# Six neighbouring tokens to a partition, mask columns by matrix product, and a new instruction order in a block-sparse attention and feed-forward kernel

## The chip, the cores and the metric

The kernel runs on one core of a Trainium2 chip. The metric is the device time of one execution in microseconds (us), taken as the median of several runs. The core has five engines that work side by side, each through its own instructions in order: TensorE (PE), VectorE (DVE), ScalarE (ACT), GpSimd (POOL) and SyncE (SP), which issues most transfers. Data lie in an on-chip memory of 128 partitions; products are summed in a second memory, PSUM.

## What is computed

Attention over 4 batches, 8 heads, 768 tokens and 64 dimensions a head, with a mask over blocks of 32 tokens, and behind it a feed-forward layer of 512 x 2048 x 512 over all 3072 tokens:

```python
block = 32; n_blocks = S // block                     # 24
scores = np.matmul(q, k.transpose(0, 1, 3, 2)) / np.sqrt(D)
mask = np.abs(blk_i - blk_j) <= 1                     # neighbours
mask = mask | (blk_i == 0) | (blk_j == 0) | (blk_i == n_blocks - 1) | (blk_j == n_blocks - 1)
for qb in range(n_blocks):
    for kb in sampled_blocks[qb]:                     # three drawn blocks per row of blocks
        mask[qb*block:(qb+1)*block, kb*block:(kb+1)*block] = True
attn = softmax(np.where(mask, scores, -1e9))
x = (attn @ v).transpose(0, 2, 1, 3).reshape(B * S, H * D)
h = x @ w_in
out = (h * sigmoid(beta * h)) @ w_out
```

## The kernel before, in words

**Loads.** Two heads form a pair, so there are 16 pairs, four per batch; x numbers them. For each pair the loads of k, q and v bring 2 x 768 rows of 64 float32 values into staging tiles `st_k`, `st_q`, `st_v` (384 KB each, `add_load`, line 473). The 768 tokens of a batch are split into three groups of 256 (`NG`), and in each group partition p gets the two neighbouring tokens 2p and 2p + 1 (`CG = 2`). A partition thus reads runs of 2 x 64 x 4 = 512 bytes. Token chunk c (of `NC = 6`, 128 tokens each, one per partition) is the even or odd half of a group. All orders within a batch follow these chunks: the columns of the transposed k and q (`kX`, `qX`), those of x, and the rows of the output that one store writes (`add_store`, line 784).

The first four pairs are loaded in pieces: pair 0's k in three parts (k0a, k0b, k0c), every q in a first part of 256 tokens (q0 to q3) and a rest of 512 (r0 to r3, two transfers each). The order on SP is fixed by `ORDER` (line 128): k0a q0 k0b k0c v0 k1 q1 v1 k2 q2 v2 k3 q3 v3 r0 r1 r2 r3. The weights w_in and w_out come in two halves each through POOL's queue (`add_weights`, line 443); the first half of w_in is held back until k3 has landed. The loads of pair 4 (k4, q4, v4) wait for halves of w_out.

**Casts and transposes.** Staged tiles are cast to float16 by DVE or POOL (`add_cast`, line 504). k and q are then transposed by PE, with a copy from PSUM by DVE or ACT (pairs 0 to 3), or by a transposing transfer from SP (later pairs).

**Units of attention.** A unit is one pair with 256 or 512 queries; there are 32, in the order of tiles of a batch. For a unit, PE forms the scores of key chunks into `sc`, ACT takes the exponential into `et` (tiles of 128 x 1024), DVE multiplies by the mask (`mk` in `tile_steps`, line 608), PE forms the product with v (`av`), DVE normalizes into `xst`. A multiply leaves out the columns of blocks of queries that see every key. In the first four units (`N_PEMASK`) PE adds the mask instead, by a product of `onehot` with `shut_qk`, and there is no multiply. x is transposed to `x` by PE in the first eight units and by transfers later.

**Mask.** `emit_first` (line 320) and `add_mask` (line 366) build a 24 x 24 table of blocks, `mask16`, from `sampled_blocks`. PE multiplies it with the identity; ACT spreads the 24 columns to 384 in `shut_qk`; DVE copies the 24 x 24 table to `mask_t`; three products with `onehot` give `mask_kb` (128 x 72); and three copies ("spread") repeat each column into `mask01` (128 x 3 x 384), which the multiplies read.

**Feed-forward.** Seven groups of tokens (256, five of 512, 256): hidden products `hp`, tanh on ACT (`t_sb`), a multiply on DVE (`g`), output products, copies or sums into `osb`, stores. Six groups use a scheme of seven products on sums of quarter matrices (`add_mixed`), for which DVE makes sums `s` and mixed weights `w_mix`.

**Order.** All instructions are emitted in the order of the string `STEPS` (line 42), one word per node: the node's number, its engine (P, A, D, G for POOL, S for SP) and the buffers it takes; "2V7" stands for two dummy products of 512 columns into bank 7 and W for 64 columns. A planner outside the kernel found this order with the durations that stand in the `add` calls. Those numbers do nothing at run time. Each engine runs its nodes strictly in this order, and waits wherever data or buffers aren't there.

Of the kernel before, what the change touches and what calls it, by code (L numbers as in the profile page):

```python
# [10 lines left out]
FP32 = mybir.dt.float32  # L11
FP16 = mybir.dt.float16
# [11 lines left out]
class Node:  # L24


    def __init__(self, kind, eng, dur, lat, emit, deps=(), take=(), use=(), moved=0,
                 rows=128, port=False, at=0.0, place=0.0, part=0, lanes=1):
# [14 lines left out]
11S0 15S0 19S 23S 27S0 12D0 0D 29S1 13P0 2V7 3W7 33S1 14A0 37S1 16D0 17P1 39S2 9P0 20G 1P2 1V7  # L43
43S2 10D 2A 3D 18D 4P3 24D 21P0 80P2 22D 5D 25P2 82P3 81A0 8G 26D 84P0 28D0 83A1 47S0 85A2
49S3 30D1 53S0 34G1 31P6 7G 35P7 86P0 32D1 36A 91P1 87D0 38D1 93P2 92A3 88D0 57S1 95P3 40D2
89P1 59S1 44D2 94A4 41P0 45P2 42D2 63S2 46A 90D0 96A5 48G2 102P2 104P1 6D 103A6 97P6 50D3 75G
105A7 54D0 51P7 76G 98D1 67S0 55P4 99D1 106P0 52D3 77G 56D 107A8 113P1 115P3 60D1 114A9 100P0
71S1 117P2 64D2 116Aa 61P1 101D 108P2 62D 68G0 118Ab 184P3 58G3 109D2 187P0 110D2 69P3 185Ac
190P2 78G 70D 65P2 111P3 188Ad 66D 193P3 79G 119P2 191Ae 186D 196P0 189D 194A0 199P2 112D
120D3 192D 197A1 210P3 121D3 195D 122P3 200A2 213P0 123D 198D 216P1 211A3 124P4 201D 127P5  # L50
214A4 212D 202P6 125A0 130P7 215D 128A1 205P0 217A5 203D4 126D0 129D 133P1 204D4 131A2 136P4
206D5 218D 134A3 219P1 137A4 139P5 207D 220A6 132D 142P0 138D 145P6 135D 140A5 72D1 148P4
143A6 141D 151P1 146A0 144D 222P1 149A1 147D 73P0 152A2 150D 154P5 223A7 74D 157P4 221D 225P3
155A4 224D 160P0 158A3 226A8 163P2 153D 159D 166P3 156D 208P1 161A5 227D 247P3 236G0 164A6
169P4 167A0 162D 237S 228P5 209D1 248A9 168D 165D 250P0 170A1 229D6 231P3 249D 251Aa 171D
253P3 230D0 232D7 256P0 254Ab 233D 259P2 172P2 252D 257A0 255D 178P3 260A1 258D 262P3 240G2
281P0 367D 173P 263A2 244G0 241S 363D 284P2 282Ac 245S 368D 287P3 179P 364D 285Ad 238D0 174P
283D 288Ae 239S0 264D 290P0 293P2 261D 296P3 291A3 175P 273S1 289D 294A4 234P0 265P1 242D0
176A0 292D 243S 180P 297A5 295D 181P 286D 276S0 298D 279S1 268P2 182A1 266D8 246G0 235D 307S2
267D1 299P6 269D9 365D 302P3 274G1 300Da 270D 301D2 404P2 303Db 275S1 407P0 304D 271P2 405A6  # L60
305P3 272D 410P3 306D 408A7 177S 413P2 369D 315P2 366D 411A8 318P3 409D 316A2 277D2 321P6
414A0 406D 278S 317D1 280G1 416P0 319A3 419P2 324P7 415D 322A4 310S1 313S0 308G2 417A1 323D
327P2 412D 309S2 420A2 330P6 418D 325A5 320D 333P0 429S3 328A0 326D 432S2 336P1 331A6 329D
334A1 437P2 421D 440P1 337A2 339P7 332D 311G1 438A9 335D 422P6 312S 338D 441Aa 342P0 423Dc
371D0 340A4 443P2 424D3 343A3 446P1 439D 345P1 444Ab 341D 430G3 348P6 442D 346A5 431S3 344D
314G2 449P2 447A3 351P7 445D 435S1 450A4 354P0 448D 349A0 347D 433G0 452P1 352A6 462P2 350D
425P1 434S 453A5 353D 357P6 451D 355A1 426Dd 360P7 454D 463Ac 427D 465P1 356D 358A2 428S2
468P2 455P1 361A4 359D 466Ad 458P0 362D 456De 469Ae 471P3 457D4 474P1 459Df 464D 377P1 472A0
460D 372D 477P2 475A1 380P0 473D 470D 478A2 487P3 490P1 476D 381P 488A6 479D 493P2 467D 491A7
496P3 378P 374D 494A8 375D 480P2 370D 379A0 483P3 497A3 481Dg 382D 499P2 482D0 388P 484Dh  # L70
500A4 485D 502P3 593P1 596P2 503A5 385P 594A9 386P 597Aa 599P3 606P1 619S0 622S0 625S0 623G2
436G3 620D0 492D 495D 498D 501D 504D 489D 389P 600Ab 383D 505P4 607A0 376D 373D 609P3 387A
612P1 506D0 508P5 595D 610A1 507D1 391P 601D 613A2 509D1 510D 627P3 640S1 183S 643S1 461S 486S
646S1 641G1 630P1 598D 628Ac 633P2 392P 384D 631Ad 390D1 644G1 602P6 634Ae 394P 603D2 626D0
604D2 648P1 661S2 621S0 664S2 511S 624S 667S0 393D 651P2 654P3 649A3 642S1 395P 635D 608D
652A4 512P2 396D 655A5 662D2 515P3 665D0 513A3 669P2 682S3 605S0 672P3 516A5 518P0 514D0 645S
517D 521P2 519A0 632D 663S2 670A6 650D 524P3 653D 685S0 397P 522A6 520D 683G3 525A1 523D 527P4
526D 666S 530P0 614D 528A2 629D 673A7 398P 401S 611D 531A4 675P1 399D 690P3 533P5 676A8 532D
403S 684S3 671D 691A9 615P1 677D 693P1 534A3 529D 686G2 696P3 636P0 694Aa 535D 536P4 647D1
697Ab 616D3 668D2 539P5 687S 692D 537A5 617D3 703P1 656D 540A0 706P3 542P1 538D 704A0 674D  # L80
545P4 543A6 637D4 560D0 548P2 638D4 546A1 544D 639S 551P3 549A4 541D 554P0 561D 688S1 552A2
547D 402S 707A1 557P1 550D 709P2 555A3 553D 716P3 657P2 558A5 556D 710A2 559D 678P3 658D5
717Ac 659D0 719P0 679D6 722P2 566P2 680D1 720Ad 563D 698D 567P 723Ae 695D 810P3 564D 813P0
816P2 811A3 569P3 721D 711D 814A4 699P6 568D1 689G3 817A5 570P 700D7 708D 819P0 701D2 822P2
705D 825P3 820A6 574P 571D 823A7 724D 712P0 573D 826A8 577P 713D8 714D4 572D 835P2 860S0 400S
863S1 702S 660S 866S0 838P3 841P0 718D 836A9 578P 562D 839Aa 827D 725P4 579D0 864G1 842Ab 575P
726D9 861G0 727D2 844P3 847P0 824D 850P2 845A0 583P 565D 576A 815D 584P 848A1 812D 580P 843D
851A2 821D 868P3 893S1 715S 681S 896S2 862S0 728S 618S 871P0 894D1 874P2 869Ac 581P 899S1 818D
897G0 872Ad 828P6 582D 875Ae 831P7 585D 829Da 849D 877P0 880P2 729P3 832Db 878A3 830D0 833D
732P6 879D 730A6 881A4 586P 731D1 852D 733A0 883P0 901P2 926S2 834S1 895S1 840D 735P3 884A5  # L90
927D2 734D 902A6 738P7 867D0 587P 736A1 885D 737D 904P0 588A 907P2 846D 741P6 739A4 592S 882D
929S0 744P3 740D 742A2 898S 837D 747P2 745A3 743D 591S 905A7 853P7 746D 590S 932S0 870D 750P6
748A5 928S2 854Dc 855D4 856P3 751A6 876D 589S 753P7 908A8 873D 865S 749D 910P0 754A0 913P2
752D 756P2 911A0 930D2 857Dd 759P6 858D 914A1 903D 762P3 755D 757A1 777D0 760A4 765P4 763A2
758D 768P5 766A3 761D 771P2 906D 769A5 767D 774P7 772A6 764D 886P4 773D 775A0 770D 916P0
1015P1 1040S3 1041G3 887De 889P6 917A2 776D 900G1 1042S3 783P5 1016A9 890Df 912D 931S 1018P0
909D 1021P1 784P 1019Aa 888D1 780D 859S 1022Ab 786P4 918D 891D 785A0 1024P0 781D 892S 1027P1
1030P3 1025A3 915D 787P 782D 1043S1 1028A4 919P0 778D 1031A5 922P1 920Dg 921D2 1048P1 923Dh
1051P3 924D 791P 1049Ac 788D 925S 1026D 1052Ad 1054P0 1057P1 1023D 794P 1055Ae 1050D 792P 790D
1058A0 1044G0 1060P3 793D 1063P0 1073P1 1061A1 933G2 795P 1045S 1020D 1064A2 934P6 1029D  # L100
1074A6 1032D 937P7 1053D 935A1 940P2 938A4 936D0 943P3 941A3 779D 1076P0 942D 944A2 946P6
1077A7 945D 949P2 1017D 947A6 952P3 789D 950A5 1075D 955P0 953A0 948D 1033P1 796D1 956A1 939D
# [899 lines left out]
```

## Time and profile before

| | |
|---|---|
| three runs | 267.02, 267.15, 277.67 us; median 267.15 |
| profiled execution | span 268.4 us from first to last instruction; the profile gives no other time of it |
| mean granted TensorE clock | 0.991 |
| busy in 0 to 25 us | PE 17.39, DVE 12.35, ACT 16.06, POOL 8.30 |
| busy in 25 to 44 us | PE 18.30, DVE 17.32, ACT 17.44, POOL 2.25 |
| 384 KB loads, issue to landing (median) | k 4.4, q 4.1, v 4.1 us |
| 128 KB parts of q | 5.4 us |
| halves of w_in, w_out | 12.4, 13.1 us |
| packets of SP's queue | 69744, 32.06 MB, 50.2% of 16 engines' span |
| last matmul ends | 264.7 us |

In the lines of the profile a group is named by its operation and its tiles, "out<-in"; in brackets stands how long the engine was idle before it and which engine, tile or transfer ended that. Nearly all instructions carry line 186, that of a helper which records them, so groups are told apart by their tiles. POOL's casts have line 510 and loads lines 481 and 484.

### The profile page before, as it was taken

What the parts mean: (1) busy time and instruction counts of PE and PEld (TensorE: products, weight loads), DVE (VectorE), ACT (ScalarE), POOL (GpSimd) and SP (SyncE); (2) the same over time, 40 slices, a digit from 0 to 9 for tenths busy, and PEclk for the clock granted to TensorE, in tenths of its full rate; (3) what the DMA queues carried; (4) which work ended last, traced back from release to release, by engine and by line L of the source; (5) the groups of instructions that cost most, each with busy time, mean ns of one, the idle gap of its engine ahead of it and who ended that gap; (6) DMA issues with size and microseconds to landing.
All of it is one profiled execution on the core that took longest, in us unless ns stands there. A gap on an engine that the chain in (4) does not pass through costs nothing.

```text
span 268.4 us, 6856 instructions
## 1 busy us (share of the span) xinstructions
PE 254.6 (95%) x2774; PEld 166.2 (62%) x2774; DVE 233.1 (87%) x492; ACT 209.7 (78%) x277; POOL 33.0 (12%) x49
## 2 busy tenths in 40 slices
PE   7793899999999899999999999999999999999994
PEld 3672675463456575646776546655667875578883
DVE  5662899999999999999998999999999788986582
ACT  3894899959999888899899898997478988564420
POOL 3234001021603200201201002020000000000000
PEclk9998899999999999999999999999999999999999
DMA  6999995297949779928189496620016012102042
GB/s 191 297 242 215 209 222 142 58 255 187 217 109 288 155 172 212 210 50 254 23 215 169 123 256 104 139 41 0 32 53 176 15 7 84 26 2 78 2 156 78
DMA packets 72978, 36.68 MB, mean 137 GB/s; under 512 B 29796, under 2 KB 68980, under 8 KB 72948
## 3 DMA queue, kind: packets, MB, share of 16 engines
q1 hardware_dynamic: 69744, 32.06, 50.2%
q0 software_dynamic: 3136, 4.19, 9.0%
q8 instruction: 21, 0.34, 0.5%
q14 instruction: 9, 0.07, 0.1%
q10 hardware_dynamic: 68, 0.01, 0.0%
HBM read 27.27 MB, written 6.29 MB: 125 GB/s over the span
## 4 chain that ended last, share of the span: by engine, by line
PE 75%; DVE 16%; DMA 3%; ACT 2%; SPq 1%; issue 1%; POOL 0%; DVEq 0%; POOLq 0%
PE sc L186 75%; DVE et L186 6%; DVE g L186 4%; DMA st_q<-in_q_dram 3%; DVE xst L186 2%; ACT et L186 1%; SPq L484 1%; DVE s L186 1%; DVE w_out_sb L186 1%; DVE recip L186 1%; DVE osb L186 0%; POOL s_q L510 0%; DVE s_k L186 0%; ACT shut_qk L186 0%; DVE s_q L186 0%
## 5 line engine op out<-in xcount | busy, mean ns | idle before, releaser
L186 ACT ACTIVATE et<-sc 128x1024 f16<-128x1024 f32 x144 | 139.8, 1037 | 19.9 <-PE sc L186 19.1
L186 PE MATMUL sc<-x,w_in_sb 128*128 128x512 f16 (+1 forms) x448 | 90.8, 349 | 0.4 <-ACT et L186 0.2
L186 ACT ACTIVATE t_sb<-sc,beta_c_sb 128x512 f16<-128x512 f32 (+1 forms) x112 | 67.6, 647 | 22.4 <-PE sc L186 19.6
L186 DVE TENSOR_TENSOR et<-et,mask 128x960 f16<-128x960 f16 (+1 forms) x132 | 83.2, 660 | 1.2 <-ACT et L186 1.0
L186 DVE SCALAR_TENSOR_TENSOR g<-t_sb,sc 128x512 f16<-128x512 f16 (+1 forms) x112 | 63.5, 603 | 2.7 <-ACT t_sb L186 2.4
L186 PEld LDWEIGHTS <-w_in_sb 128*128 128x128 f16 x448 | 41.5, 98 | 38.0 <-issue 6.1
L186 PEld LDWEIGHTS <-g 128*128 128x128 f16 x483 | 45.4, 98 | 17.3 <-issue 7.5
L186 PE MATMUL sc<-w_out_sb,g 128*128 128x256 f16 (+1 forms) x384 | 51.2, 282 | 0.0
L186 PE MATMUL sc<-qX,kX 64*128 64x256 f16 (+1 forms) x384 | 46.2, 329 | 0.7 <-DVE qX L186 0.3
L186 PEld LDWEIGHTS <-et 128*128 128x128 f16 x1152 | 41.4, 98 | 7.5 <-issue 2.8
L186 PE MATMUL sc<-va,et 128*128 128x65 f16 x1152 | 43.6, 194 | 0.6 <-ACT et L186 0.3
L186 PEld LDWEIGHTS <-kX 64*128 64x128 f16 x384 | 16.0, 94 | 17.8 <-issue 13.3
L186 PE MATMUL sc<-w_mix,s 128*128 128x256 f16 x176 | 22.2, 273 | 0.7 <-DVE osb L186 0.7
L186 DVE TENSOR_TENSOR xst<-sc,recip 128x256 f16<-128x256 f32 x48 | 19.9, 418 | 0.8
L186 PEld LDWEIGHTS <-s 128*128 128x128 f16 x176 | 16.2, 98 | 5.5 <-issue 3.4
L186 DVE TENSOR_TENSOR osb<-osb,sc 128x512 f32<-128x512 f32 (+1 forms) x18 | 11.3, 635 | 6.1 <-ACT osb L186 3.2
L186 ACT COPY osb<-sc 128x512 f32<-128x512 f32 (+2 forms) x16 | 9.0, 562 | 9.2 <-PE sc L186 7.9
L510 POOL CAST s_q<-st_q 128x768 f16<-128x768 f32 (+2 forms) x10 | 9.6, 960 | 50.5 <-DMA st_q<-in_q_dram 37.7
L510 POOL CAST s_k<-st_k 128x768 f16<-128x768 f32 (+1 forms) x8 | 7.0, 877 | 51.0 <-DMA st_k<-in_k_dram 51.0
L186 DVE RECIPROCAL recip<-sc 128x4 f32<-128x4 f32 x48 | 8.3, 175 | 5.1 <-PE sc L186 4.8
L510 POOL CAST va<-st_v 128x768 f16<-128x768 f32 x9 | 9.3, 1029 | 23.4 <-DMA st_v<-in_v_dram 23.4
L186 PE MATMUL sc<-w_mix,g 128*128 128x256 f16 x88 | 11.1, 272 | 0.0
(65 smaller groups left out, 107.6 us busy)
## 6 DMA issues: line engine op xcount, KB each, us to landing
st_v<-in_v_dram SPq DMA_DIRECT2D x16, 384.0 KB, 4.1
out_dram<-osb SPq DMA_DIRECT2D x23, 256.0 KB, 2.3
st_k<-in_k_dram SPq DMA_DIRECT2D x15, 384.0 KB, 4.4
st_q<-in_q_dram SPq DMA_DIRECT2D x12, 384.0 KB, 4.1
w_in_sb<-in_moe_w_in_dram POOLq DMA_DIRECT2D x2, 1024.0 KB, 12.4
w_out_sb<-in_moe_w_out_dram POOLq DMA_DIRECT2D x2, 1024.0 KB, 13.1
st_q<-in_q_dram SPq DMA_DIRECT2D x12, 128.0 KB, 5.4
st_k<-in_k_dram SPq DMA_DIRECT2D x3, 128.0 KB, 2.4
```

The lines of the kernel that those rows point to most:

```text
L186: r = f(*a, **kw)
L484: nc.sync.dma_start(out=o[:, g::NG], in_=hg[:, g::NG])
L510: e(out=at(dst)[:, :, :, 0:D] if nm == "v" else by_chunk(dst, lo, hi), in_=src)
```

## The change

A partition gets six neighbouring tokens of a batch, 6p to 6p + 5, and chunk c is the c-th of them. A full load so reads one run of 1536 bytes per head and partition; a part of two chunks 512, and a rest of four chunks 1024 bytes in one transfer instead of two. Chunks 2g and 2g + 1 of a partition lie in the same block of 32 tokens, so the mask is a function of partition and g (`onehot[:, g]`).

`onehot` is made by POOL in token order in a scratch tile and copied by DVE into the order of g. The product of `mask16` is now with `onehot` itself and gives 384 columns; from it come `shut_qk` (128 columns, as only g = 0 is needed) and `mask_q` (24 x 384), and three products of `onehot` with `mask_q` give the three parts of `mask01`, copied from PSUM by ACT or DVE. `mask_t`, `mask_kb` and the spreads go. A multiply leaves out the first and last four partitions' queries in every chunk: 120 of 128 columns, so 960 elements for 256 queries (before 896) and 960 for 512, with a further level in the access pattern.

Stores write the rows of one chunk, each 2048 bytes, at a distance of six tokens instead of two.

`STEPS` is new throughout. Node numbers rise by one behind the mask. In the new order 19 casts go from DVE to POOL, two from POOL to DVE, eight PSUM copies of the output from DVE to ACT and two from ACT to DVE.

The diff also brings code for splitting products into two halves of the rows (`halves`, `products`, the branches on `HALVED` and `HALVED_AV`). Both switches are empty, and none of it is emitted.

```diff
-11S0 15S0 19S 23S 27S0 12D0 0D 29S1 13P0 2V7 3W7 33S1 14A0 37S1 16D0 17P1 39S2 9P0 20G 1P2 1V7
-43S2 10D 2A 3D 18D 4P3 24D 21P0 80P2 22D 5D 25P2 82P3 81A0 8G 26D 84P0 28D0 83A1 47S0 85A2
...
+12S0 16S0 20S 24S 28S0 0D 30S1 21G 34S1 17D0 5V7 2W7 1P0 13G0 18P1 25G 38S1 3A 14P2 2A 3W7 26P3
+15D0 22P4 40S2 19A 27D 6P5 23A 8P6 29D0 7A 44S2 85P0 9A 83P1 48S0 86A0 10P7 31D1 50S3 4P4 35D1
...
+HALVED_AV = False
+HALVED = ()
...
             nc.gpsimd.tensor_copy(
-                out=onehot[r].rearrange("b g (m r) -> b (g m) r", r=BLK // CG),
+                out=onehot_n[r].rearrange("b p g -> b (p g)").rearrange(
+                    "b (m r) -> b m r", r=BLK // CG),
...
+        nc.vector.tensor_copy(out=onehot, in_=onehot_n.rearrange("b p g -> b g p"))
...
-            pe.matmul(at(tb)[:, 0:NB], lhsT=mask16.rearrange("b h j -> b (h j)"),
-                      rhs=identity[0:NB, 0:NB], start=True, stop=True)
+            pe.matmul(at(tb)[:, 0:NG * P], lhsT=mask16.rearrange("b h j -> b (h j)"),
+                      rhs=onehot[0:NB].rearrange("b g p -> b (g p)"), start=True, stop=True)
...
-            copy_on(eng)(out=mask_t, in_=at(tb)[0:NB, 0:NB])
...
+            copy_on(eng)(out=mask_q, in_=at(tb)[0:NB, 0:NG * P])
+
+        def km(g, kb):
+            pe.matmul(at(kb)[:, 0:NG * P], lhsT=onehot[0:NB, g], rhs=mask_q, start=True, stop=True)
+
+        def kmc(eng, g, kb):
+            copy_on(eng)(out=mask01[:, g], in_=at(kb)[:, 0:NG * P])
...
-        def spread(eng, g):
...
-            hg = src[b, 2 * j:2 * j + 2].rearrange("h (g p c) d -> p (h g) (c d)", g=NG, p=P)
-            o = at(st).rearrange("p h (g c) -> p (h g) c", g=NG)
-            if hi - lo == NC:
-                nc.sync.dma_start(out=o, in_=hg)
-            else:
-                for g in range(lo // CG, hi // CG):
-                    nc.sync.dma_start(out=o[:, g::NG], in_=hg[:, g::NG])
+            rows = src[b, 2 * j:2 * j + 2].rearrange("h (p c) d -> p h (c d)", c=NC)
+            nc.sync.dma_start(out=at(st)[:, :, lo * D:hi * D], in_=rows[:, :, lo * D:hi * D])
...
-        lo, hi = BLK // CG * (q0 == 0), n // CG - BLK // CG * (q0 + n == S)
-        masked = 2 * CG * kn * (hi - lo)
+        lo, hi, ng = 4, P - 4, n // (CG * P)
+        masked = 2 * CG * kn * ng * (hi - lo)
...
-                e = at(et).rearrange("p h (r q) -> p (h r) q", q=w)[:, :, lo:hi]
-                m = mask01[:, kc0 // CG, q0 // CG + lo:q0 // CG + hi].unsqueeze(1).to_broadcast(
-                    [P, 2 * CG * kn, hi - lo])
+                e = at(et).rearrange("p h (r g q) -> p (h r) g q", g=ng, q=P)[:, :, :, lo:hi]
+                m = mask01[:, kc0 // CG, q0 // CG:(q0 + n) // CG].rearrange(
+                    "p (g q) -> p g q", q=P)[:, :, lo:hi].unsqueeze(1).to_broadcast(
+                        [P, 2 * CG * kn, ng, hi - lo])
...
-            rows = out[b * S:(b + 1) * S, :].rearrange("(g p c) m -> g c p m", p=P, c=CG)
-            nc.sync.dma_start(out=rows[c // CG, c % CG][:, m0:m0 + w],
+            rows = out[b * S:(b + 1) * S, :].rearrange("(p c) m -> c p m", c=NC)
+            nc.sync.dma_start(out=rows[c][:, m0:m0 + w],
```

More of the change, by code (lines that the diff above doesn't have):

```diff
@@ L27, in __init__ @@
     def __init__(self, kind, eng, dur, lat, emit, deps=(), take=(), use=(), moved=0,
-                 rows=128, port=False, at=0.0, place=0.0, part=0, lanes=1):
+                 rows=128, port=False, at=0.0, place=0.0, part=0, lanes=1, cross=None,
+                 packet=512):
+        self.packet = packet
+        self.cross = -1 if cross is None else cross.no
         self.kind, self.place, self.part, self.lanes = kind, place, part, lanes
@@ L49 @@
[L49 to L54, printed above, removed]
@@ L304, in emit_zeros, with halves @@
                       rhs=warm[:, 0:w], start=True, stop=True)
+    def halves(phase, a, b):
+        lo, hi = slice(0, P // 2), slice(P // 2, P)
+        for x, y in zip(a, b):
+            for (buf, out, lhs, rhs, start), r in zip((x, y), (hi, lo) if phase else (lo, hi)):
+                Tap.into = buf
+                pe.matmul(out, lhsT=lhs(r), rhs=rhs(r), start=start and not phase, stop=True,
+                          skip_group_check=True)
+        Tap.into = None
     log = []
@@ L641, in add_tail @@
         last = None
-        for half in range(nq // 2):
+        for half in range(0 if HALVED_AV else nq // 2):
             ab, rb = Buf("mm"), Buf("recip")
@@ L666, in nm @@
                     out=at(xs)[:, half * 2:half * 2 + 2], in0=av_ap()[:, :, :, 0:D],
[L667 to L670 removed]
+                    in1=at(rb)[:, 0:2].to_broadcast([P, 2, 2, D]), op=ALU.mult)
```

411 lines of the change are left out of this document (251 added, 160 removed).

## The prediction

> **What bounds the kernel now.** I read the page first (engine shares, chain), then the chain in order of time, then windows, the early timelines, and the DMA queues.
>
> ```profile
> PE 254.6 (95%) x2774; PEld 166.2 (62%) x2774; DVE 233.1 (87%) x492; ACT 209.7 (78%) x277; POOL 33.0 (12%) x49
> ```
>
> TensorE is the bound over the whole, but not everywhere. The chain in order of time is PE from 97.8 to 264.7 us, DVE from 57 to 98, and before 24 us it is a load. The windows (PE, PEld, DVE, ACT, POOL busy, then clock, DMA share, GB/s) say the same:
>
> ```profile
> 16.00:20.30 4.30, 3.90 (x64) 2.54 (x60) 2.69 (x9) 4.13 (x6) 0.67 (x1) 1.00 1.13 210
> 20.30:24.40 4.10, 0.06 (x3) 0.05 (x2) 0.03 (x1) 1.78 (x2) 0.71 (x2) 1.00 1.13 217
> ...
> 25.00:28.40 3.40, 3.40 (x38) 2.23 (x38) 2.37 (x7) 2.05 (x2) 1.77 (x3) 0.53 1.14 219
> ```
> ```profile
> 58.00:98.00 40.00, 38.68 (x412) 21.82 (x411) 39.72 (x75) 37.98 (x49) 10.96 (x10) 1.00 0.88 200
> 98.00:130.00 32.00, 32.00 (x350) 20.04 (x346) 30.51 (x61) 29.03 (x37) 4.86 (x5) 1.00 0.67 160
> ```
>
> The one large hole is at 20.3 to 24.4 us: PE does 0.06 us of work, while DMA is full. Its cause, from the timelines of PE, POOL and ACT:
>
> ```profile
> 24.36 0.40 PE L186 MATMUL sc<-identity,s_q 128*128 128x128 f16 x4 [4.04 <-POOL s_q L510]
> ```
> ```profile
> 15.01 1.66 POOL L451 DMA_DIRECT2D w_in_sb<-in_moe_w_in_dram  x2 [0.31 <-POOL w_in_sb L462]
> 23.69 0.61 POOL L510 CAST s_q<-st_q 128x512 f16<-128x512 f32 x1 [7.02 <-DMA st_q<-in_q_dram]
> ```
> ```profile
> 6.80 2.85 ACT L186 ACTIVATE et<-sc 128x1024 f16<-128x1024 f32 x3 [1.28 <-PE sc L186]
> ...
> 25.28 1.02 ACT L186 ACTIVATE et<-sc 128x1024 f16<-128x1024 f32 x1 [3.20 <-PE sc L186]
> 26.63 1.02 ACT L186 ACTIVATE et<-sc 128x1024 f16<-128x1024 f32 x1 [0.33 <-PE sc L186]
> 28.52 2.85 ACT L186 ACTIVATE et<-sc 128x1024 f16<-128x1024 f32 x3 [0.86 <-PE sc L186]
> ```
>
> PE stands in line at the transposes of r2 (the rest of pair 2's q). Behind them wait the scores of pairs 0 and 1, whose data are there; so ACT, busy from 6.8 us on, runs dry. r2 is late because both w_in transfers, issued at 15.01, share the DMA engines with it. Queue lines, 8 to 16 us, then 17 to 24 us (q1 SP's loads, q0 weights):
>
> ```profile
> DMA packets 4681, 2.34 MB, mean 292 GB/s; under 512 B 145, under 2 KB 4680, under 8 KB 4680
> ```
> ```profile
> q0 software_dynamic: 569, 1.14, 91.0%
> q1 hardware_dynamic: 557, 0.27, 18.5%
> ```
>
> Alone, 512-byte rows move at 292 GB/s; beside the weights the queues alternate one packet for one, so the loads fall to 0.27 MB in 7 us. By the packet records r2's last row starts at 22.07, r3's at 29.16.
>
> **The change, part by part.** *Loads.* Row times in the packet records (median): 512 B 27 ns, 1024 B 47, 2048 B 85. No row shows 1536 B; its bounds are 66 ns (midway) and 81 (no gain per byte), and I take 66, as the three rows lie on a line. A 384 KB load is then 16 rows per engine, 1.06 us for 1.35 (at 292 GB/s). k0's three parts and q0 to q3 keep 512-byte rows; r0 to r3 get 1024-byte rows, 0.75 us for 0.9, and one issue each for two. The last rows start today at 4.1 (k0c), 13.07 (k3), 14.9 (v3). Six full loads to k3 save 0.29 each: 11.3. v3 12.9, r0 13.6, r1 14.4, r2 15.1. Weights start 3.7 us after k3's last row (16.80 against 13.07), so at 15.0: r2 is through. With no gain per byte: v3 14.9, r1 16.4, weights at 16.8, r2's last two thirds at 85 rows per us: 18.5. Both are well before 22.07.
>
> *POOL's queue.* The order puts only the first w_in transfer behind k3; the second follows the casts of v3 and r2, and w_out follows r3's cast. So r3 meets one transfer: 16 rows per engine and 16 weight rows of 172 ns: 3.5 us, landing near 19. The second w_in is issued near 17.5 and queues behind the first (16.80 to 23.41 now, hence about 15 to 21): DMA stays full, and all weights end near 39 for 40.85. If r2 came late, the w_in and w_out transfers would queue behind its cast; the cover is the 3 us until the first ends.
>
> *PE's order.* r2's transposes move behind all of unit 4's scores, two units' transposes and the first of unit 5. The 4.04 us wait goes, and ACT's three waits with it: 3.20 + 0.33 + 0.86 = 4.4 us. What is late next is ACT itself: 18 exps at 0.904 start to start.
>
> The half clock at 25.0 to 28.4 should go too; I count nothing more for it, since ACT's waits of 0.33 and 0.86 are in the sum. (If ACT were not last there, it would be worth 1.6: 3.4 us at 0.53.)
>
> *Mask.* Removed: a 24-column product, `mask_t` (0.17), `mask_kb` (0.22), three spreads (POOL 0.51 twice, DVE 0.46). Added: one 128x384 DVE copy of `onehot` that waits for POOL's two copies (end 2.79) and holds DVE's va memsets and the mask bits; products of 384 columns; PSUM copies of 384 columns, three on ACT (0.49 each, the row of `shut_qk`), one on DVE. `shut_qk` shrinks to 128 columns (0.27). The mask bits end at about 4.5 for 4.26; ten dummy products instead of seven keep PE until about 5.0 (0.43 each cold, 0.22 after 4.3). Then ACT, in order: mask copy, shut_qk, two transposed copies at 0.37, two mask copies: the first exp at 7.7 for 6.80. k0a's cast, now on POOL behind k0b's, ends near 5.1 and is not last. Bounds 0.4 and 1.5 later; taken 0.9, and it lies on the path, as ACT bounds this stage. One transposed copy (0.3) fewer on ACT later.
>
> *Mask multiplies.* 36 of 132 grow from 896 to 960 elements, all in tiles of 256 queries:
>
> ```profile
> L186 DVE TENSOR_TENSOR et<-et,mask 128x960 f16<-128x960 f16 x96 | 62.0, 674 | 1.2 <-ACT et L186 1.0
> ...
> L186 DVE TENSOR_TENSOR et<-et,mask 128x896 f16<-128x896 f16 x36 | 21.2, 621 | 0.0
> ```
>
> Start to start 0.569 against 0.535: 36 x 0.034 = 1.2 us of DVE. They lie at 96 to 135 and past 210 us, beside PE at 100%: nothing, or 1.2 if DVE were last there. The 96 others read 8 runs of 120 instead of 4 of 240; the 896 form has 8 runs of 112 already, at the same rate, so nothing.
>
> *Casts to POOL.* 19 casts go from DVE to POOL and 2 come back. Saved per 768-column cast: 0.47 us. Against it:
>
> ```profile
> 58.87 0.68 DVE L186 TENSOR_TENSOR w_mix<-w_out_sb,w_mix 128x1024 f16<-128x1024 f16 x1
> 59.47 1.33 DVE L186 TENSOR_TENSOR w_out_sb<-w_out_sb 128x1024 f16<-128x1024 f16 x1
> ```
>
> The same shape takes 0.65 longer while POOL casts from 59.43 on. Over the 20 POOL casts after 40 us, multiplies and sums that overlap one lost 5.8 us beyond their medians, 0.29 per cast. In 58 to 98 us, where DVE is last, two casts move: 2 x (0.47 - 0.29) = 0.4 us won. Bounds: 0.9 won if they meet nothing, 0.7 lost if each holds DVE for its whole 0.83. Eight PSUM copies move from DVE to ACT, all after 110, beside PE: nothing.
>
> [...]
>
> *SP.* k4's transpose now stands before the loads of q4 and v4, which wait for its cast; but these loads wait for w_out's second half anyway (41.6 now, about 40 then), and k4 lands before 38. Unit 8 starts at 56.7: hidden. Stores keep 2048-byte rows. The `halves` branches emit nothing (both switches empty).
>
> *Sum.* -4.4 + 0.9 - 0.3 - 0.4 = -4.2. From 98 us on PE has no hole to hold the shift back, and the 3.7 us after its last matmul (264.7) stay. The span of 268.4 becomes 264.2. The page gives that execution by its span alone, 1.3 above the median of the runs, 267.15; so 262.9.
>
> **The rivals.** *More (0.20):* the reshuffled late order also removes PE spacing and DVE's relief is whole. Loads that come sooner take ACT's earlier waits (0.39, 0.80, 0.17: 1.4), and the 1.3 us of PE idle in 58 to 98 goes: 260.2, with order gains of some 3 more 257. For it: DVE falls by some 10 us. Against: PE is at 100% after 98.
>
> *Given back (0.15):* the stall goes but a new one comes where the order was drawn tight: hp needs w_in's second half by about 29, the op products need w_out by 40, unit 8 needs q4. Each is 1 to 3 us later than a shifted schedule would like: 264.5 to 270, an eighth of it beyond 272.5.
>
> *Casts collide (0.08):* the nine casts that move to POOL between 45 and 118 us all fall on mask multiplies and hold DVE for 0.83 each where they cost it 0.47: 9 x 0.36 = 3.2 us, and DVE, last in 58 to 98, stays last until the shift is eaten: 262.9 + 0.4 + 3.2 = 266.5. For it: nine casts of POOL in that stretch took 1.1 to 1.4 us instead of 0.83, so they do meet. Against: reciprocals, normalizations and the products with tanh beside a POOL cast kept their times. [...]
>
> *Rows bring nothing (0.04):* r2 still lands near 22; PE's new order hides part: 266.
>
> *Slower (0.05):* the mask multiplies lose their rate because both operands now have another stride level. [...] Against it: 896 elements in 8 runs are at full rate.
>
> **How the numbers follow.** Forecast 0.48, own range 261 to 265. Two per cent, 5.3 us, is about what a measurement of this kernel tells from no change, so faster means under 261.8: all of More, and 0.15 out of the forecast's 0.48: 0.35. Slower: 0.05, and 0.02 of Given back. Same: the rest, 0.58. The range 258.5 to 268 leaves out about half of More's lower end (0.08), Slower (0.05) and the top of Given back (0.06).
>
> **What would show it.** Right: no PE hole over 1 us at 18 to 26, no half clock after 5 us, r2's rows before 19, full loads landing 0.3 us sooner, first exp at 7.2 to 8.3, unit 4's last exp at 26 to 27 for 30.4, multiplies still at 0.65. Wrong: PE waiting for w_in near 28, ACT idle at 8 to 18, DVE multiplies over 0.75, or PE idle after 98.

## The result and the profile after

| | before | after |
|---|---|---|
| runs beside each other | 267.02, 267.15, 277.67, 277.80 us | 277.46, 279.04, 279.17, 280.19 us |
| median | 267.1 of the first two | 279.11 |
| ratio of comparable runs, 95% | | 1.0443 [1.0379, 1.0507] |
| profiled execution | span 268.4 us | span 277.3 us (279.04 us) |

Slower by 4.4%, on the other side of the forecast of 262.9. The executions of before come in two sorts, about half with spans of 263.4 to 265.6 us and the others of 266 to 277 us; the profile that the prediction rests on (268.4) is of the second sort, and the ratios go by the shorter executions. A time lies about 1.9 us above its span in these runs, so that execution took an estimated 270.3 us, 3.2 us more than the median.

The page, busy us and share of each engine:

```profile
PE 258.2 (93%) x2778; PEld 167.2 (60%) x2778; DVE 233.6 (84%) x466; ACT 214.0 (77%) x288; POOL 48.2 (17%) x64
```

TensorE does 3.6 us more work in a span that is 8.9 us longer; VectorE has 26 instructions fewer and is as busy as before. The windows (PE, PEld, DVE, ACT, POOL busy, clock, DMA share, GB/s), with those that the prediction showed:

```profile
16.00:20.30 4.30, 4.18 (x90) 3.60 (x88) 2.54 (x8) 4.30 (x6) 2.41 (x3) 1.00 0.97 185
20.30:24.40 4.10, 3.29 (x40) 1.57 (x41) 3.01 (x10) 3.89 (x5) 0.00 (x0) 1.00 1.12 222
25.00:28.40 3.40, 3.02 (x28) 2.01 (x27) 2.90 (x6) 3.40 (x7) 1.33 (x2) 1.00 1.10 207
44.00:58.00 14.00, 10.15 (x136) 5.90 (x136) 10.51 (x21) 7.42 (x11) 4.78 (x6) 1.00 0.82 233
58.00:98.00 40.00, 39.45 (x406) 22.22 (x404) 38.46 (x68) 38.08 (x48) 11.04 (x11) 0.96 0.49 130
98.00:130.00 32.00, 28.34 (x297) 16.89 (x296) 28.50 (x50) 26.10 (x34) 9.82 (x10) 1.00 0.87 193
```

The kernel before in 44 to 58 us, which the prediction did not show:

```profile
44.00:58.00 14.00, 13.61 (x158) 7.21 (x155) 13.71 (x29) 11.10 (x14) 2.13 (x2) 1.00 0.59 137
```

The old hole at 20.3 to 24.4 us is gone (3.29 us busy for 0.06). Two new ones stand at 44 to 58 (3.9 us idle, where before had 0.4) and at 98 to 130 (3.7 us idle, before none). The 0.96 in 58 to 98 is half clock from 58.0 to 61.4, right behind the first. ScalarE's timeline shows the part of the forecast that came true:

```profile
8.17 1.97 ACT L191 ACTIVATE et<-sc 128x1024 f16<-128x1024 f32 x2
11.03 2.85 ACT L191 ACTIVATE et<-sc 128x1024 f16<-128x1024 f32 x3 [0.89 <-PE sc L191]
...
14.42 9.41 ACT L191 ACTIVATE et<-sc 128x1024 f16<-128x1024 f32 x10
```

Ten exps run without a gap, and the next four behind one of 0.18 us, where before stood the waits of 3.20, 0.33 and 0.86 us. By the packet records r2's last row starts at 17.79 us (22.07 before), and unit 4's last exp ends at 26.9 (30.5). The rows of 1536 bytes, for which no figure was there, take 65 ns (median) where 66 was forecast.

The hole at 44 to 58 ends in this line of TensorE's timeline (in brackets the idle time, and what ended it); the line behind it is the whole run's sum, times and longest of that wait:

```profile
57.41 0.61 PE L191 MATMUL sc<-qX,kX 64*128 64x512 f16 x4 [3.08 <-DMA qX<-s_q]
```
```profile
PE sc L191 <- DMA qX<-s_q: 5.6, 3, 3.1
```

TensorE waits for the transposed q of pair 4, with which unit 8 begins. Its path back runs through POOL (timeline):

```profile
27.07 0.95 POOL L510 CAST s_q<-st_q 128x512 f16<-128x512 f32 x1 [7.11 <-DVE et L191]
27.97 1.76 POOL L460 DMA_DIRECT2D w_out_sb<-in_moe_w_out_dram  x2
38.23 0.18 POOL L491 CAST st_k<-w_out_sb 1x1 f32<-1x1 f16 x1 [8.51 <-DMA w_out_sb<-in_moe_w_out_dram]
44.47 1.05 POOL L510 CAST s_k<-st_k 128x768 f16<-128x768 f32 x1 [6.06 <-DMA st_k<-in_k_dram]
45.47 0.61 POOL L491 CAST st_q<-w_out_sb 1x1 f32<-1x1 f16 x1
...
50.85 1.33 POOL L510 CAST s_q<-st_q 128x768 f16<-128x768 f32 x1 [4.21 <-DMA st_q<-in_q_dram]
```

and through SP:

```profile
45.55 1.32 SPq L525 DMA_TRANSPOSE kX<-s_k  x1
47.04 0.45 SPq L485 DMA_DIRECT2D st_q<-in_q_dram  x1
...
52.21 1.21 SPq L525 DMA_TRANSPOSE qX<-s_q  x1
```

Read from the end: q4's transpose is issued at 52.21 and TensorE starts 5.2 us later; four loads were put into the same queue ahead of it (48.05 to 50.05). It waits for q4's cast at 50.85, that for q4's load, issued at 47.04. The load waits for its gate, the one-element copy at 45.47, and on SP for k4's transpose. The gate's own condition, w_out's second half, was met at 43.9; it stands in POOL's queue behind k4's cast, which waited 6.06 us for k4. The kernel before has these lines on POOL:

```profile
25.01 1.76 POOL L454 DMA_DIRECT2D w_out_sb<-in_moe_w_out_dram  x2
35.83 0.18 POOL L490 CAST st_k<-w_out_sb 1x1 f32<-1x1 f16 x1 [9.06 <-DMA w_out_sb<-in_moe_w_out_dram]
41.43 0.17 POOL L490 CAST st_q<-w_out_sb 1x1 f32<-1x1 f16 x1 [5.42 <-DVE g L186]
```

There k4's cast was VectorE's, and both gates passed at 41.4 to 41.7, right behind w_out's second half (41.3). So of the 4.0 us by which q4's gate is late, 2.5 are w_out's, which is issued behind r3's cast, at 27.97 instead of 25.01, and some 1.6 are the place behind k4's cast.

In that profile of before, q4's transpose was issued no earlier (52.60), because VectorE came to k4's cast only at 49.29. In b_again2, a profile of the same kernel without the first hole (below), it came there at 45.67, the transpose was issued at 49.00, and unit 8's first exp came at 54.0 us, for 57.1 in the first profile and 57.8 in the changed kernel. The queues so took back what the first 40 us had won.

### The profile page after: what moved, and what is told of

Same layout as the page of the kernel before. It is cut to its first block, busy times and chain, and to the rows that moved or that the text cites. A ratio compares the mean times of both kernels' runs of the same rounds, so it can differ in the third digit from the quotient of the medians.

```text
span 277.3 us, 6836 instructions
## 1 busy us (share of the span) xinstructions
PE 258.2 (93%) x2778; PEld 167.2 (60%) x2778; DVE 233.6 (84%) x466; ACT 214.0 (77%) x288; POOL 48.2 (17%) x64
## 4 chain that ended last, share of the span: by engine, by line
PE 57%; DVE 18%; DMA 14%; ACT 5%; SPq 2%; issue 2%; POOL 1%; DVEq 0%; POOLq 0%; ACTq 0%
PE sc L191 57%; DVE et L191 6%; DVE g L191 5%; DMA st_k<-in_k_dram 4%; DMA qX<-s_q 4%; DMA w_out_sb<-in_moe_w_out_dram 4%; ACT et L191 3%; DVE xst L191 2%; DMA st_q<-in_q_dram 2%; ACT t_sb L191 1%; SPq L485 1%; SPq L525 1%; DVE s L191 1%; POOL s_q L510 1%; DVE recip L191 1%
## 5 line engine op out<-in xcount | busy, mean ns | idle before, releaser
L191 DVE TENSOR_TENSOR et<-et,mask 128x960 f16<-128x960 f16 x132 | 89.1, 710 | 6.6 <-ACT et L191 6.1
L191 ACT ACTIVATE t_sb<-sc,beta_c_sb 128x512 f16<-128x512 f32 (+1 forms) x112 | 65.5, 635 | 24.8 <-PE sc L191 22.9
L191 DVE SCALAR_TENSOR_TENSOR g<-t_sb,sc 128x512 f16<-128x512 f16 (+1 forms) x112 | 64.3, 605 | 8.3 <-ACT t_sb L191 7.8
L191 PE MATMUL sc<-qX,kX 64*128 64x512 f16 (+1 forms) x384 | 46.7, 329 | 8.5 <-DMA qX<-s_q 5.6
L191 PE MATMUL sc<-va,et 128*128 128x65 f16 x1152 | 43.9, 194 | 1.6 <-DVE et L191 1.3
L510 POOL CAST s_q<-st_q 128x768 f16<-128x768 f32 (+2 forms) x15 | 15.2, 1011 | 38.5 <-DMA st_q<-in_q_dram 29.5
L510 POOL CAST s_k<-st_k 128x768 f16<-128x768 f32 (+1 forms) x15 | 13.0, 875 | 50.6 <-DMA st_k<-in_k_dram 50.6
L191 ACT COPY osb<-sc 128x512 f32<-128x512 f32 (+2 forms) x22 | 12.2, 555 | 9.9 <-PE sc L191 8.5
L510 POOL CAST va<-st_v 128x768 f16<-128x768 f32 x14 | 13.8, 987 | 33.6 <-PE sc L191 21.3
L191 PE MATMUL sc<-w_mix,g 128*128 128x256 f16 x88 | 10.8, 273 | 0.0
## 6 DMA issues: line engine op xcount, KB each, us to landing
w_in_sb<-in_moe_w_in_dram POOLq DMA_DIRECT2D x2, 1024.0 KB, 10.8
```

What stands on the lines that cost most here:

```text
L191: r = f(*a, **kw)
L510: e(out=at(dst)[:, :, :, 0:D] if nm == "v" else by_chunk(dst, lo, hi), in_=src)
```

## The experiments

The order is a list of steps: node number, engine (P, A, D for VectorE, G for POOL, S for SP) and slot. Numbers are those of the changed kernel: 73 r3's cast, 79 and 80 w_out, 237 k4's gate, 239 its cast, 240 its transpose, 241 and 245 the gates of q4 and v4, 242 and 246 their loads, 243 and 244 q4's cast and transpose. Ratios are against the kernel before on the same chip.

### Order or layout

**e1_new_rows_old_order** translates the old order to the new nodes. The added mask steps had to be placed by hand:

```diff
-84A1 48S0 86A2 50S3 31D1
+84A1 48S0 86A2 6P0 50S3 31D1
...
-54S0 35G1 7G 32P6 36P7
+54S0 35G1 7D 32P6 36P7
```

> The changed loads (six tokens to a partition) and the changed mask, in the order of the kernel before: the same engine for every step, the same queues, two mask copies on VectorE in the places where the old spreads stood. Theory ORDER (the 12 us are lost in the order drawn anew; rows and mask by themselves gain a little): 261 to 267 us, r2's last row near 19.5 us instead of 22.07, TensorE 13.5 us or more busy of 14 in 44 to 58 us, no half clock near 58 us. Rival LAYOUT (the rows, or what the mask multiplies read, cost the time in any order): 275 us or more.

Measured: 1.0323 [1.0187, 1.046], a profile of span 272.3. TensorE is 13.99 of 14 us busy in 44 to 58 and 31.65 of 32 in 98 to 130, so neither new hole is there; but half clock stands at 12.4 to 15.8 and at 26.1 to 32.9, and r2's last row starts at 24.56 us, not near 19.5. The product `6P0` waited 1.75 us at 10.8 for unit 0's exps, which still held its bank. Neither theory had that: the new mask, placed like this, does not fit the old order's first 25 us.

**e2_old_rows_new_order** is the reverse.

> The reverse: rows and mask of the kernel before, in the order of the changed kernel. ORDER: 277 to 285 us, since the loads are slower on top, with the same two holes in TensorE's work as in the changed kernel (44 to 58 us and 98 to 130 us). LAYOUT: 268 us or less.

Measured: 1.051 [1.0433, 1.0588], TensorE 8.96 of 14 and 28.28 of 32 us in the two stretches. Both holes come with the order, whatever the rows and the mask.

**h1_old_start** repeats e1 with a free bank for the two products and w_in's second half (78) behind r2's cast (69):

```diff
-42P0 46P2 43D2 64S2 47A
+42P0 46P2 43D2 6P0 64S2 47A
...
-104A6 98P6 51D3
+104A6 98P6 8P1 51D3 9D
...
-78G 69G0
+69G0 78G
```

> Rows and mask of the change, the order of the kernel before nearly throughout: w_in's second half is issued behind r2's cast, as in the changed kernel, and the second and third mask product stand where their bank is free and nothing waits behind them (in e1 one stood behind unit 0's exps). Theory ORDER: level with the graft at 26 us or up to 1 us ahead, since unit 0's first exp comes at 7.0 to 7.8 us: 265 to 267.5 us. Rival LAYOUT (rows and mask cost a few us unless the order is fitted to them): 269 us or more.

Measured: 1.0226 [1.0126, 1.0325]. ORDER failed again and LAYOUT's sentence for this run holds: in the old order rows and mask cost some 6 us. They are lost in the first 25 us again: unit 3's exps end at 24.1 us, against 19.8 to 20.9 in every kernel that starts in the new order. In this profile full clock begins only at 13.1 us, and r0's rows run from 18.0 to 22.8, beside w_in's; TensorE's longest wait, 2.17 us, is for the cast behind that load:

```profile
24.02 0.43 DVE L188 CAST s_q<-st_q 128x512 f16<-128x512 f32 x1 [3.44 <-DMA st_q<-in_q_dram]
```

h2_five_casts_pool (below) has the same order over this stretch. In its profile full clock begins at 5.3 us and r0's rows end at 15.6, and unit 3's exps still end at 22.7. There a mask copy of VectorE's waits for its product, and q3's cast, for which TensorE then waits 0.41 us, stands behind it:

```profile
17.28 0.56 DVE L188 CAST mask<-sc 128x384 f16<-128x384 f32 x1 [1.08 <-PE sc L188]
17.76 0.28 DVE L188 CAST s_q<-st_q 128x256 f16<-128x256 f32 x1
```

From unit 9 on h1 keeps its distance to the kernel before. So the new mask needs a start drawn anew, and that part of the new order earns its place; how much of the 6 us is the mask's steps and how much the loads that follow from them is not separated.

### Where in the order

The grafts take the changed kernel's order for all steps it had begun by some time of its profile, and the old order for the rest (a few buffers change slots). r70 is the reverse: the order of g26 to 70 us, then the new one.

> A graft: rows and mask of the change throughout; the steps that the changed kernel had started by 28 us of its profile, in its order, and all others in the order of the kernel before (on its engines, in its queues; six buffers take another slot of their pool). e1 had lost its time ahead of 25 us alone (a mask product that I had placed stood behind unit 0's exps), and ran level with the kernel before from there. Theory ORDER: the early gain of the changed kernel (unit 5's exps end at 36.2 us instead of 40.3) is kept to the end: 262.5 to 265.5 us. Rival LAYOUT (the columns that the mask multiplies now read, or the wide rows, cost time later in any order): 268 us or more. Rival ABSORBED (the early gain is lost where w_out or the loads of pair 4 bound unit 8, at 57 us, whatever the order): 266 to 268.

> The same graft at 26 us: r3's cast is then VectorE's again, and both halves of w_out are issued right behind w_in, near 20 us. ORDER with w_out early: unit 8's loads about 2 us earlier than in the graft at 28 us, but w_in shares the DMA engines with w_out and TensorE waits for w_in near 26 us as in e3 (1.6 us, with half clock): 263 to 267 us, 0 to 2 us behind the graft at 28 us. Rival (the wait for w_in was bad luck of e3): 0.5 to 2 us ahead of the graft at 28 us.

> The graft at 56 us: the changed kernel's order up to and with the hole at 44 to 58 us, and the order of the kernel before behind it. It prices the two halves of the loss: theory ORDER says that the part behind 58 us (the hole at 98 to 130 and the one near 165) is worth 5 to 8 us: 271 to 274 us, TensorE 31 us or more busy of 32 in 98 to 130. Rival LAYOUT: 276 us or more, since rows and mask are as in the changed kernel.

> The graft at 36 us (the changed kernel's order for all steps begun by then, the order of the kernel before from there). Theory LATE PREFIX (the first loss lies in what the new order does between 36 and 56 us: the gates, casts and loads of pairs 4 to 7): 266.5 to 269 us. Rival EARLY PREFIX (it lies ahead of 36 us: w_out behind r3's cast, and the products of group 0 drawn ahead): 272 to 276 us.

> The graft at 44 us. k4's gate and load are passed by then, its cast and the gates of q4 and v4 are not, so they stand in the old order again. LATE PREFIX with the cause in POOL's and SP's queues behind 44 us: 266.5 to 269.5 us. Rival UNIT ORDER (the new order has taken TensorE's and ScalarE's work of units 6 and 7 ahead, so nothing is left to fill the wait for q4): 271 to 275 us, with TensorE idle at 50 to 57 us.

> The reverse graft: the order of the graft at 26 us for all steps begun by 70 us of its profile, and the changed kernel's order from there. Theory TWO LOSSES (the late one, 274.9 to 279.1 us in the graft at 56 us against the changed kernel, stands by itself): 270 to 272.5 us, with TensorE idle for 2 us or more in 98 to 130. Rival ONE LOSS (the late holes come from loads that the first hole delayed): 266.5 to 268.5 us.

| kernel | new order | ratio, 95% |
|---|---|---|
| g26_w_out_early | to 26 us | 1.0002 [0.9975, 1.0028] |
| g28_new_start_old_order | to 28 us | 1.0033 [0.9992, 1.0073] |
| g36 | to 36 us | 1.0063 [1.0029, 1.0097] |
| g44 | to 44 us | 1.0077 [1.0051, 1.0104] |
| g56_late_old_order | to 56 us | 1.0302 [1.0258, 1.0345] |
| changed kernel | all | 1.0443 [1.0379, 1.0507] |
| r70 | from 70 us | 1.0224 [1.0196, 1.0252] |

With 267 us to 1.00 this is the account of the 11.8 us: 0.1 for rows, mask and the new start; 2.0 between 26 and 44 us; 6.0 between 44 and 56; 3.8 behind 56 us. The rows were measured on more than one chip, each against the kernel before beside it, and by their intervals the last three terms are good to about 1.0, 1.4 and 2.1 us. The 6.0 hold the half clock that follows the hole (6.8 us of it in g56's profile, 3.4 in the changed kernel's). By itself the late part costs 5.9 (r70 against g26). Windows of g44 and g56 at 44 to 58:

```profile
44.00:58.00 14.00, 13.82 (x160) 7.42 (x159) 13.48 (x29) 10.18 (x12) 3.03 (x4) 1.00 0.84 208
```
```profile
44.00:58.00 14.00, 8.53 (x125) 5.32 (x123) 10.75 (x21) 6.19 (x8) 6.81 (x8) 1.00 0.81 229
```

What stands between the two in POOL's and SP's queues (g44 first):

```diff
-237G0 241G2 245G0 247G0
+237G0 239G0 241G2 245G0 243G0 247G0
...
-238S 242S 246S 240S0 274S1 244S 277S0 280S1 308S2
+238S 240S0 242S 246S 274S1 277S0 280S1 308S2 244S
```

The casts of k4 and q4 go to POOL, the gates fall behind the first of them, and three more loads ahead of q4's transpose. LATE PREFIX holds, and in g44, where units 6 and 7 are drawn ahead as in the changed kernel, UNIT ORDER falls. For the late part, g26 and r70 in 98 to 130:

```profile
98.00:130.00 32.00, 31.53 (x333) 19.12 (x331) 31.53 (x59) 28.79 (x37) 4.65 (x5) 1.00 0.62 151
```
```profile
98.00:130.00 32.00, 29.68 (x303) 17.74 (x299) 28.22 (x50) 27.40 (x36) 9.21 (x10) 1.00 0.76 168
```

TWO LOSSES holds: the late one stands without the first. g56 has no late hole (31.78 us busy in 98 to 130), yet its 275.1 us lie above ORDER's 271 to 274: the late part is worth 3.8 us there and not 5 to 8. ORDER failed for g28 and g26 in a point that matters: both are level with the kernel before and not 2 to 4 us ahead.

### Was the forecast gain there?

**b_again** and **b_again2** are the kernel before, unchanged, for another profile.

> The kernel before, profiled once more. Most of its runs beside the experiments had spans near 264.5 us at a clock of 0.997 to 1.00; the profiled execution that the prediction rests on had 268.4 us. Theory TYPICAL (the hole at 20.3 to 24.4 us and its half clock belong to the longer executions): span 263.5 to 265.5, no half clock ahead of the end, and TensorE more than 6.2 us busy of 9 in 16 to 25 us instead of 4.56; then most of the forecast gain was never there to be had. Rival: the hole of about 4 us with its half clock is there again, and the span is 267 to 269.

> The kernel before a third time, for a profile of one of its usual executions (spans of 264 to 265.6 us at a clock of 0.997 or more). Theory TYPICAL: in such a profile TensorE has no wait of 4 us for q3's second load near 20 us, is 6.2 us or more busy of 9 in 16 to 25, and unit 5's exps end at 36 to 38 us. Rival CLOCK ALONE: the hole of 4 us stands in it as well and only the half clock behind it is missing: TensorE 4.5 to 5 us busy of 9, and unit 5's exps end at 38.5 us or later.

b_again has span 270.8, the wait of 4.0 us again, r2's last row at 23.45. b_again2 has span 266.2, and its window over the hole is:

```profile
20.30:24.40 4.10, 3.41 (x46) 1.89 (x44) 3.71 (x10) 4.10 (x6) 2.23 (x3) 1.00 1.12 215
```

No hole: TensorE 3.41 us busy for 0.06, 7.81 of 9 in 16 to 25. r2's last row starts at 18.78, unit 4's exps end at 25.9 and unit 5's at 37.3 (40.3 in the first profile). TYPICAL holds; this profile has 3.4 us of half clock in 25 to 44 and is still 2.2 us shorter than the first. Three profiles do not say how often the hole comes.

### What in the first hole

**e5_gates_only** and **e3_early_queues**; e3 has the whole edit, e5 all but the first pair of lines (w_out's issues):

```diff
-113D 73G2 71D 101P0 198A2 79G 214P1
+113D 79G 80G 73G2 71D 101P0 198A2 214P1
...
-239G0 230D6
+241G2 245G0 239G0 230D6
...
-254P1 240S0 179P4 245G0 286A0 265D 180P 242S
+254P1 242S 246S 240S0 179P4 286A0 265D 180P
```

> The changed kernel with six steps of POOL's and SP's queues moved: both halves of w_out are issued ahead of r3's cast, the gates of q4 and v4 ahead of k4's cast, and the loads of q4 and v4 ahead of k4's transpose. Theory QUEUE (the hole at 44 to 58 us is q4 waiting behind k4's cast, and w_out behind r3's): w_out's first half lands near 36 instead of 38.2 us, q4's last row near 44 to 46 instead of 49.9, TensorE 13 us or more busy of 14 in 44 to 58, no half clock behind 58, and 273 to 275.5 us. Rival CONTENTION (the loads of pair 4 are late because the weights hold the DMA engines): q4's last row stays behind 48 us and the time is 278 to 280. Rival ABSORBED (unit 8 comes early but the time is lost again at 98 to 130): 277 to 279 with TensorE full in 44 to 58.

> The changed kernel with four steps moved: the gates of q4 and v4 ahead of k4's cast on POOL, and the loads of q4 and v4 ahead of k4's transpose on SP. w_out stays behind r3's cast. Theory QUEUE: the gates alone make the hole at 44 to 58 us, and e3's early issue of w_out cost it something at 25 to 44 (TensorE waited 1.6 us for w_in and half clock followed): here q4's last row near 45 to 46 us, TensorE 18.4 us busy of 19 in 25 to 44 and 12.5 or more of 14 in 44 to 58, and 270 to 273 us. Rival W_OUT (what helped e3 was w_out's earlier issue): 276 to 279.

e3: 1.0235 [1.0168, 1.0301], 5.6 us won; q4's last row starts at 45.41 (49.90) and TensorE is 13.66 of 14 us busy in 44 to 58. That is QUEUE on each count but one: w_out's first half landed at 37.35, not near 36. e5: 1.0343 [1.0295, 1.0391], 2.7 us won, less than expected (10.86 of 14 us busy), and its 276.2 us lie in W_OUT's range. By the middle values the gates are about half and w_out, which QUEUE had only named, the other half; the intervals leave about 2 us to either. In e5 the gates pass at 44.3, when w_out's second half has landed, and q4's transpose, issued at 49.91, comes 6.2 us ahead of TensorE's start: it stands behind four loads.

**e6_q4_path** mends that too, in e3:

```diff
-274S1 277S0 280S1 243G0 308S2 244S
+243D0 244S 274S1 277S0 280S1 308S2
```

> The kernel of e3 (early queues mended) with q4's path cleared further: its cast on VectorE instead of POOL, and the loads of k5, q5, v5 and k6 behind q4's transpose on SP instead of ahead of it. Theory QUEUE: q4's transpose waits in the DMA queue behind those loads (issue to TensorE's start 6.1 us in e5, 4.7 in the graft at 28 us): unit 8's first exp at 52.5 to 54.5 us instead of 56.0 in e3, TensorE 13.7 us or more busy of 14 in 44 to 58, and 270 to 272.5 us. Rival ABSORBED: unit 8 comes sooner but unit 9 and later wait for their own loads, which are now later: 273 to 275.

Unit 8's first exp comes at 53.2 (56.0 in e3), as expected, yet the ratio is 1.0354 [1.0292, 1.0417], 3.2 us worse than e3. ABSORBED holds and falls short: 58 to 98 us in e3 and e6.

```profile
58.00:98.00 40.00, 37.94 (x410) 22.11 (x408) 38.90 (x72) 37.90 (x48) 7.30 (x7) 1.00 0.56 139
```
```profile
58.00:98.00 40.00, 36.25 (x389) 20.82 (x390) 37.36 (x68) 34.86 (x44) 11.14 (x10) 0.96 0.54 139
```

Unit 9's exps start no earlier (66.9 for 66.6): the loads of pairs 5 and 6 now come later (k5's is issued at 47.64 for 45.87, its transpose at 58.92 for 56.38). The wait, mended singly, moved to the next step of the same queue.

### What in the second hole

**e4_late_casts_dve** changes one letter in eleven steps (`621G0` to `621D0`; also 627, 648, 663, 666, 669, 868, 895, 928, 931, 1048).

> The changed kernel with eleven casts from pair 13 on given back from POOL to VectorE, at the same places in the order. Theory HEAD OF LINE (the hole at 98 to 130 us is casts that wait in POOL's queue behind others, and transposes and loads behind them in SP's): TensorE 31 us or more busy of 32 in 98 to 130 instead of 28.3, and 273 to 276 us. Rival VECTORE (VectorE is what bounds that stretch, and each cast put back costs it 0.9 us): 280 to 287 us. Rival SP (the order of SP's own loads and transposes makes the hole, whoever casts): 278 to 281 us, with the hole still there.

Measured: 1.0389 [1.0293, 1.0484], a gain of 1.4 us that the interval does not separate from none; TensorE 29.69 of 32 us in 98 to 130 for 28.34. HEAD OF LINE in this form is worth, by its middle value, a third of the late 3.8 us, and VECTORE falls: eleven more casts on VectorE, 6.6 us of them, cost no time.

**h2_five_casts_pool** is the reverse in h1, `278D2` to `278G2` and 621, 627, 648, 663 likewise.

> h1 with five casts (q6, k13, v13, v14, k15) on POOL as the changed kernel has them, at their old places. Theory RELIEF (VectorE bounds 58 to 98 us, and loses 0.47 us per cast less): 0.5 to 1.5 us ahead of h1. Rival COLLISION and HEAD OF LINE (the casts slow the mask multiplies beside them, and transposes wait for POOL): 0.5 to 3 us behind h1, with TensorE idle at 98 to 130.

Measured: 1.019 [1.0126, 1.0254], not to be told from h1's; by its middle value it would be 1.0 us ahead, as RELIEF had it. But from unit 8 to unit 12, its profile falls behind g26's by 1.7 us more (62.2 against 60.0, then 93.8 against 89.9; both have the old order there but for these casts; h2's stretch holds 3.4 us of half clock). That speaks against RELIEF, but between two profiles only; the times decide nothing here.

**r70_loads** and **e3_loads** move five loads of pairs 13 and 14 on SP:

```diff
-429S2 462S 487S 620S0 623S1 626S1 641S2 644S0
+429S2 620S0 623S1 626S1 641S2 644S0 462S 487S
```

> r70 with five loads (k13, q13, v13, k14, q14) moved ahead on SP, in front of the output transposes of units 9 and 10, where the order of the kernel before has them; nothing else changes. Theory LOADS (they are issued 12 us late, and TensorE runs dry at 93 to 118 us): issued by 76 to 80 us, TensorE 0.5 us or less idle between 94 and 112, and 268.5 to 270.5 us. Rival POOL (v13's cast waits for the products of an earlier unit until 98 us, and k14's and q14's casts behind it): 271.5 to 273 us with the loads early.

> The kernel of e3 (the changed kernel with six steps of POOL's and SP's queues moved) with the same five loads moved ahead as well: eleven moved steps in all, no engine changed. If LOADS holds and the two mends add: 269.5 to 272 us, against 273.4 for e3 and 279.1 for the changed kernel. If POOL holds: 272.5 to 274 us.

Measured: 1.0211 [1.0118, 1.0304] and 1.0230 [1.0177, 1.0283]: no gain on r70 (1.0224) or e3 (1.0235). k13's load is issued at 77.0 instead of 88.0 us, and it does not help. LOADS falls. POOL's timeline in r70_loads shows what the pairs wait for next:

```profile
97.39 1.05 POOL L507 CAST va<-st_v 128x768 f16<-128x768 f32 x1 [14.44 <-PE sc L188]
98.38 0.83 POOL L507 CAST s_k<-st_k 128x768 f16<-128x768 f32 x1
99.14 1.26 POOL L507 CAST s_q<-st_q 128x768 f16<-128x768 f32 x1
```

v13's cast stands 14.4 us at the head of POOL's queue, until TensorE has read the buffer it is to fill; k14's and q14's, whose loads landed at 84.7 and 85.8, wait behind it, and their transposes, the loads behind those on SP and the casts of pair 15 follow from there. POOL is what the trace shows, but no run took v13's cast out of the queue alone, and e4, which did so among others, won little. How the late 4 to 6 us divide between POOL's order, SP's and the units' stays open.

## Why the prediction was wrong

**The step that failed** is the paragraph on SP: "k4's transpose now stands before the loads of q4 and v4 ... but these loads wait for w_out's second half anyway (41.6 now, about 40 then), and k4 lands before 38. Unit 8 starts at 56.7: hidden." Its cover was two dates that were not followed through POOL's queue. w_out hangs on r3's cast, which I had near 19 and which came at 27.07. For r3's load waits for the buffer that r0's cast frees, and was issued at 18.5 (18.3 before); it landed at 26.92, and the bracket of the cast's line names VectorE only because an instruction there ended 0.07 us later. So w_out's first half came at 38.2, k4's load left only then and landed at 44.4, not before 38. And the gates of q4 and v4, which I took to wait for w_out alone, stand behind k4's cast on POOL. The step was to be 0 us; by the grafts it is 6.0, and 2.0 for the part ahead of 44 us.

**"From 98 us on PE has no hole to hold the shift back"** is the second. It was read from the old order for a new one. r70 prices it at 5.9 us alone, 3.8 behind the first loss.

**-4.4 us for r2.** The mechanism was right in place and size for the profiled execution: wait gone, half clock there gone, unit 4 3.6 us earlier. What failed is the base. In b_again2 r2's last row starts at 18.78 without the change, so an execution like that had nothing to give, and g26, with the new start and without the losses, is at 1.0002. I set the profiled execution 1.3 us above the median, its span against a time; by the estimate above it stood 3.2 above.

**+0.9 for the start.** 1.4 in the changed kernel's profile (8.17 for 6.80); 0.3 to 1.4 over the profiles with that start, for bounds of 0.4 and 1.5. It is about made up by unit 3, whose exps end at 19.8 to 20.9 for 20.2.

**-0.4 for casts.** No relief: VectorE is busy 233.6 us, as before. The mask multiplies were to stay at 0.65 us:

```profile
L191 DVE TENSOR_TENSOR et<-et,mask 128x960 f16<-128x960 f16 x132 | 89.1, 710 | 6.6 <-ACT et L191 6.1
```

They take 89.1 us for 83.2 (62.0 and 21.2), and eat more than half of the casts' ten. The 106 that overlap no cast of POOL did stay: their mean is 653 ns (before 114 with 638, 32 of the smaller 36 among them). The 26 that overlap one take 942 (before 18 with 801). By these means the new columns and the larger 36 cost some 2 us and POOL's casts some 4.6 more than before. e4, the same order with eleven casts fewer on POOL, takes 86.5. What slows a multiply beside a cast, no run shows.

**The rivals.** Given back named the very place ("unit 8 needs q4") at 0.15, and priced it at 1 to 3 us because only one late wait was counted, not the queue behind it and not the late part. Slower named the wrong cause: the multiplies kept their rate wherever no cast of POOL met them (653 ns for 638). Casts collide had it right that they are slower beside a cast (942 ns), but its 3.6 us would not have made the loss. Rows bring nothing fell for the profiled execution and is true of b_again2.

**What was to show it:** "PE idle after 98" stood among the signs of being wrong, and was the right one to list.

## What to carry to other kernels

An engine's queue is a chain of its own (k4's cast, which waited 6.06 us, held q4's gate some 1.6 us beyond its own condition): when a step moves to another engine, write down what now stands behind it there and what that waits for, and follow the last date through every queue, DMA issues and one-element gates included. A wait that is hidden "anyway" is hidden only if its cover keeps its date in the new order. And ask for a second profile of the kernel before when its runs differ: a gain read from one execution may not exist in the others.

## What was not expected of the hardware

- **Half a microsecond went with more than three.** By the packet records w_in's first row follows r2's first by 0.10, 0.27 and 0.56 us in the three profiles of the kernel before; r2's rows then take 5.4, 5.9 and 2.1 us. In the changed kernel the distance is 0.66 and they take 1.8. Once the weights' rows were under way, the load's rows stood among them (557 to 569 in 17 to 24 us of the profile before).
- **A late issue left a gap in the DMA engines' work.** w_in ends at 29.9 us and w_out is issued at 27.97, but in 28.4 to 31.0 the engines move 74 GB/s, against 205 in the same window of the kernel before, where w_out was issued at 25.01. Part of that is the time from issue to first row: 1.58 us for w_out, and 1.89 for w_in in the same profile. What the rest of the gap is, no run shows.
- **Half clock followed little work, not only none.** By the clock and matmul records it lasted 3.41 us, or twice that, except at the end of the span, and began on a grid of 3.41 us: in the profile before, full clock runs from 4.30 to 24.78 and from 28.19 to 267.13 us, six and seventy times 3.413. In the 3.41 us ahead of it TensorE was busy, by matmul records of which a few per cent can be missing, for 0.42 us (before), 0.59 (after), 1.22 and 1.57 (e1), 1.31 (h1's order with h2's casts), 1.63 (e3) and even 2.17 (b_again2). Stretches of the same grid with 1.61 (e2), 1.85 (g56) and 2.01 us (after) were not followed by it, and all windows below 1.6 in these traces were. Between 1.6 and 2.2 us both happened; what decided there, no run shows.
- **A transpose queued behind loads.** From its issue to TensorE's start q4's took 5.2 us behind four loads (after), 6.2 behind four (e5) and 4.0 behind one (g44).
